# From the search on, every compute engine takes the program's order, laid out along a clock of products

## The chip, the cores and the metric

The kernel runs on one core of a Trainium2 chip. The metric is the device time of one execution in microseconds (us). The core's engines are TensorE (matrix products and transposes; PE in the profile, its weight loads PEld), VectorE (DVE), ScalarE (ACT), GpSimd (POOL) and SyncE (SP, which issues most transfers). Each has a queue of its own and they meet through semaphores.

## What is computed

Attention with 4 sink keys and a window of 128 keys (batch 4, 8 heads, 768 positions, head size 64) gives 3072 tokens of 512 numbers. A dense layer follows, and then a layer of eight experts. Cut to that:

```
h = x @ w_in                      # 512 -> 2048
x = (h - np.tanh(h)) @ w_out      # 2048 -> 512
logits = x @ w_gate               # one for each of 8 experts
# all (token, expert) pairs, greatest logit first:
#   give the token to the expert if the token is free and the expert has under 384
out[mask_e] = np.maximum(x[mask_e] @ w1[e], 0) @ w2[e]    # 512 -> 1024 -> 512
```

So each expert gets exactly 384 tokens, and which ones depends on all logits.

## The kernel before, in words

**Ahead of the change.** Tokens are handled in 8 units of 384. Attention and the dense layer run unit by unit, the second product of a unit beside the next unit's attention. Every fp32 operand of a large product is split into a rounded half and a remainder, and three products are summed: high by high, high by low, low by high. For the last unit, the logits are taken from the hidden values directly (`last_logits`, L476; `logits`, L434 to L438), so that the search can start before that unit's second product (`mlp_y`, L399 to L401) is done.

**The search.** `choose` (L1025 to L1040) finds for each token its greatest logit among the experts that are left and cuts it into eight digits of four bits. `search` finds, for the expert that fills first, the value of its 384th token, a digit a level, eight levels. In a level VectorE compares the digit with 16 steps, in two halves of 12 token columns (L648, L650, tile mk); TensorE counts by expert (six products, L655, into the bank `search`); VectorE takes the counts over (L665, csum); TensorE sums and spreads them (four products, L668); VectorE finds the digit (L673 to L677). Then `assign` writes the expert's number (L704, ei), the tokens' places (L706 to L742), two offset products (L711, L712), the one-hot tile `oh` in six pieces (L753), 24 products that gather the token numbers (L757), and the list `idx` (L759, L761). The next `choose` is issued in the middle of it, right after the offset products. One expert's search follows the other, as each needs the tokens left over; the eighth expert takes what remains.

**An expert.** Its number is read on SP's queue (L769), and 16 weight loads of 256 KB follow (L775, tile wraw, 8 buffers). ScalarE rounds each (L780), GpSimd takes the remainder (L782; for some of the first expert, VectorE). There are two sets of weights, so expert n + 2 loads where n has finished. GpSimd gathers the expert's 384 rows from memory (L789, yg), TensorE transposes them in four pieces of three (L794, xt), ScalarE and VectorE split them (L797, L798, mxh and mxl). `first` makes a slice of 128 hidden values with 12 products (L830 to L832), ScalarE and VectorE make hh and hl (L835, L836), `second` adds the slice to three result banks with 9 products (L846 to L848); eight slices an expert, `second` one slice behind. Results are copied (L852) and scattered (L853).

**What sets the order.** The instructions are traced in the program's order and then ordered by a scheduler that works with its own estimate of when each is ready. The program counts a clock of products (213 ns for each of L399 to L401, 480 for three of `first`, 640 for three of `second`), and `beside` lets the search go one step on whenever the clock reaches `due`, with gaps in `GAPS`. Each step's instructions of TensorE are tied behind the product just traced, and nothing else is tied: a later product may be scheduled ahead of a search product. `weights` paces loads (a quarter of `PACE0` or `PACE` apart) and their splits (`LAT`), and `step` places the transposes by `TW` and `TR`. The search may be one expert ahead of the next (`limit = n + 2`).

```
while due <= clock and chain:
    with tc.issue_after(mm.ins):
        gap = next(chain, None)
    if gap is not None:
        due = max(due, clock - 300) + gap
```

## Time and profile before

| | |
|---|---|
| median of 3 runs | 1261.08 us (1258.85 to 1264.31) |
| the profiled execution | 1260.94 us, of it span 1259.2 us |
| mean granted TensorE clock | 0.969 |
| busy: TensorE, weight loads | 92%, 76% |
| busy: VectorE, ScalarE, GpSimd | 62%, 51%, 41% |

The span goes from the first to the last instruction; what lies around it is 1.7 us. A matmul's end is modelled and matmuls overlap, so what one costs is read from start to start and not from its duration. A busy TensorE can still be slowed by changes between kinds of products. The stage that the change touches begins near 826.8 us, where the last unit's second product starts.

### The profile page before, as it was taken

The numbers are of one execution on the slowest core, as the hardware profiler recorded it, in microseconds if no ns is written. First come the engines' busy times: TensorE is split into PE (matmuls) and PEld (weight loads), VectorE is DVE, ScalarE is ACT, GpSimd is POOL, SyncE is SP. The second block draws the span as 40 slices with busy tenths as digits, with TensorE's granted clock in tenths as the row PEclk, the third lists the DMA queues.
The fourth block names the chain that finished last, engine by engine and source line by source line (L and its number), as shares of the span: only waits on it lengthen the run. The fifth ranks groups of instructions, "written<-read, shape, count | busy, mean of one in ns | idle before, by whom it ended". The sixth has DMA issues, their size and how long they took to land.

```text
span 1259.2 us, 19625 instructions
## 1 busy us (share of the span) xinstructions
PE 1160.1 (92%) x6484; PEld 954.4 (76%) x6484; DVE 780.1 (62%) x2205; ACT 642.6 (51%) x1556; POOL 513.9 (41%) x614
## 2 busy tenths in 40 slices
PE   4667899999999999999999999997899999999797
PEld 3556688888888788888888888875577777777696
DVE  6789985566665666655656654556667666667221
ACT  6876665666665567655656654412143244143411
POOL 6266753233442434432322331002174474484920
PEclk9868899999999999999999999999889999999999
DMA  6545552234333433432333221125154145145600
GB/s 218 176 145 181 187 163 93 76 104 132 108 110 111 134 107 107 131 104 67 100 98 91 91 82 48 37 59 187 49 167 144 60 159 169 57 151 170 190 26 26
DMA packets 87605, 145.28 MB, mean 115 GB/s; under 512 B 9680, under 2 KB 32208, under 8 KB 87504
## 3 DMA queue, kind: packets, MB, share of 16 engines
q1 hardware_dynamic: 83664, 131.45, 33.2%
q0 software_dynamic: 3840, 12.59, 3.0%
q8 instruction: 51, 0.84, 0.3%
q14 instruction: 50, 0.41, 0.1%
HBM read 127.22 MB, written 16.78 MB: 114 GB/s over the span
## 4 chain that ended last, share of the span: by engine, by line
PE 65%; DMA 7%; DVE 5%; issue 4%; ACT 2%; POOL 2%; SPq 1%; POOLq 0%; ACTq 0%; DVEq 0%
PE h L373 6%; PE y L401 6%; PE h L371 6%; PE h L372 6%; PE y L399 6%; PE y L400 6%; PE o L349 4%; PE h L830 3%; PE h L831 3%; PE h L832 2%; PE o L847 2%; PE o L848 2%; PE o L846 2%; DMA wraw<-in_w_dram 2%; PE t L317 2%
## 5 line engine op out<-in xcount | busy, mean ns | idle before, releaser
L782 POOL TENSOR_TENSOR w<-wraw,w 128x512 fp32r<-128x512 f32 x120 | 152.1, 1299 | 150.5 <-ACT w L780 122.1
L371 PE MATMUL h<-xh,win 128*128 128x384 f32 x512 | 178.6, 350 | 0.3 <-ACT xh L361 0.3
L373 PE MATMUL h<-xh,win 128*128 128x384 f32 x512 | 177.3, 346 | 0.0
L372 PE MATMUL h<-xl,win 128*128 128x384 f32 x512 | 175.2, 342 | 1.7 <-DVE xl L362 1.7
L401 PE MATMUL y<-wo,gl 128*128 128x512 f32 x336 | 141.3, 422 | 0.0
L399 PE MATMUL y<-wo,gh 128*128 128x512 f32 x336 | 135.1, 404 | 1.5 <-ACT gh L384 1.5
L400 PE MATMUL y<-wl,gh 128*128 128x512 f32 x336 | 136.2, 405 | 0.1
L298 POOL TENSOR_SCALAR a<-a,stat 128x260 f32<-128x260 f32 (+2 forms) x168 | 94.2, 573 | 80.0 <-DVE stat L290 74.2
L780 ACT CAST w<-wraw 128x512 fp32r<-128x512 f32 x128 | 78.1, 620 | 87.6 <-DMA wraw<-in_w_dram 83.5
L286 ACT ACTIVATE a<-sm,stat 128x260 f32<-128x260 f32 (+2 forms) x192 | 94.5, 492 | 41.3 <-DVE stat L285 39.1
L285 DVE CUSTOM_DVE_ANT_0 sm<-s,m 128x260 f32<-128x260 f32 (+2 forms) x192 | 76.8, 401 | 50.2 <-PE s L277 41.2
L371 PEld LDWEIGHTS h<-xh,win 128*128 128x128 f32 x512 | 97.5, 191 | 7.2 <-ACT xh L361 1.2
L372 PEld LDWEIGHTS h<-xl,win 128*128 128x128 f32 x512 | 97.6, 191 | 7.0 <-DVE xl L362 2.5
L378 DVE TENSOR_TENSOR g<-h,g 128x384 f32<-128x384 f32 x128 | 71.2, 556 | 47.7 <-ACT g L377 47.0
L248 POOL TENSOR_TENSOR kl<-k,kh 128x388 fp32r<-128x388 f32 (+1 forms) x64 | 81.4, 1279 | 45.1 <-ACT kh L247 45.1
L373 PEld LDWEIGHTS h<-xh,win 128*128 128x128 f32 x512 | 97.7, 191 | 2.5 <-issue 1.5
L835 ACT ACTIVATE hh<-h 128x384 fp32r<-128x384 f32 x64 | 31.2, 489 | 132.1 <-PE h L832 119.2
L377 ACT ACTIVATE g<-h 128x384 f32<-128x384 f32 x128 | 61.9, 484 | 66.8 <-PE h L373 61.7
L262 POOL TENSOR_TENSOR vs<-vr,vs 128x192 fp32r<-128x192 f32 (+1 forms) x64 | 46.5, 734 | 113.8 <-ACT vs L261 113.1
L830 PE MATMUL h<-mxh,w 128*128 128x384 f32 x256 | 91.1, 357 | 1.7 <-ACT mxh L797 1.7
L831 PE MATMUL h<-mxl,w 128*128 128x384 f32 x256 | 90.5, 354 | 0.0
L832 PE MATMUL h<-mxh,w 128*128 128x384 f32 x256 | 89.0, 348 | 0.0
(263 smaller groups left out, 2863.1 us busy)
## 6 DMA issues: line engine op xcount, KB each, us to landing
wl<-wol_d SPq DMA_DIRECT2D x128, 256.0 KB, 2.9
wraw<-in_w_dram SPq DMA_DIRECT2D x128, 256.0 KB, 3.9
k<-in_k_dram SPq DMA_DIRECT2D x64, 131.0 KB, 2.9
winr<-in_w_in_dram SPq DMA_DIRECT2D x8, 1024.0 KB
wor<-in_w_out_dram SPq DMA_DIRECT2D x8, 1024.0 KB, 4.9
wtr<-in_w_outT_dram SPq DMA_DIRECT2D x8, 1024.0 KB, 6.1
k<-in_k_dram SPq DMA_DIRECT2D x64, 97.0 KB, 2.5
q<-in_q_dram SPq DMA_DIRECT2D x32, 192.0 KB, 2.7
```

Source lines behind the costliest of these rows:

```text
L286: nc.scalar.activation(a[:, hh, :n], sm[:, :n], AF.Exp, bias=r[:, 0, hh:hh + 1], scale=-1.0, accum_out=r[:, 1, hh:hh + 1])
L298: nc.gpsimd.tensor_scalar(a[:, j, :n], a[:, j, :n], r[:, 3, j:j + 1], 1.0, op0=OP.mult, op1=OP.mult)
L371: nc.tensor.matmul(hp, w, xh[:, c], start=(c == 0), stop=False)
L372: nc.tensor.matmul(hp, w, xl[:, c], start=False, stop=False)
L373: nc.tensor.matmul(hp, win(f, 1, c), xh[:, c], start=False, stop=(c == NC - 1))
L399: yield 213, nc.tensor.matmul(y, gh[:, ts], hi, start=(f == 0), stop=False)
L400: yield 213, nc.tensor.matmul(y, gh[:, ts], lo, start=False, stop=False)
L401: yield 213, nc.tensor.matmul(y, gl[:, ts], hi, start=False, stop=(f == NF - 1))
L782: (dve if n == 0 and q % 2 else nc.gpsimd).tensor_sub(t[:, 1], r, raw(t)[:, 0])
L830: nc.tensor.matmul(hp, w1h[:, c], xh[:, c], start=(c == 0), stop=False)
L831: nc.tensor.matmul(hp, w1h[:, c], xl[:, c], start=False, stop=False)
L832: yield 480, nc.tensor.matmul(hp, w1l[:, c], xh[:, c], start=False, stop=(c == NC - 1))
```

## The change

All instructions of TensorE, VectorE, ScalarE and GpSimd that are traced from the search's pools on are chained in the program's order, engine by engine (`in_order`); SP's are not. The program's order is now laid out by a clock in ns with a heap of events: `advance` adds a product's cost (230 for the dense second product and `second`, 175 for `first`) and runs what is due. The clock keeps for VectorE, ScalarE and GpSimd until when each is taken (`on_vec`, `on_act`, `on_pool`). A search step yields four numbers: VectorE's time beside the products just issued, the lag from those products, VectorE's time for the step, and the cost of the products that come next; the next step runs when VectorE's time is over. hl, weight halves, result copies and scatters are events as well, and in `second` the three low products come last.

A level's comparison is one instruction and no longer two. The number is written before the places are worked out. The list comes ahead of the next choice. The digits are made as 1 + d/16 by integer operations on VectorE, where ScalarE scaled them before. The rows are gathered as soon as the list is there, and the transposes are placed 9500 ns later (`GOT`), and not before 28000 ns into the running expert (`TW`); a piece may wait up to 1500 ns for a search product to stand beside. The search may run three experts ahead of the running one's number (`limit = n + 3`, where it was `n + 2`). Loads are 2000 ns apart in the dense product and 1500 after it.

```diff
-PACE0, PACE = 5000, 6000
-LAT0, LAT = 5000, 6000
-TW, TR = (16000, 14000, 12000), 2000
-GAPS = (1600, 500, 1500, 6000)
+PACE0, PACE, LAT = 2000, 1500, 6500
...
-                yield 213, nc.tensor.matmul(y, gl[:, ts], hi, start=False, stop=(f == NF - 1))
...
+                    mm = nc.tensor.matmul(y, m[:, ts], w, start=(f == 0 and w is hi and m is gh),
+                                          stop=(f == NF - 1 and m is gl))
+                    yield 230, mm
...
     psH = ctx.enter_context(tc.tile_pool(name="psH2", bufs=2, space=bass.MemoryType.PSUM))
...
+    begin = len(nc.cur_bb.bb.instructions)
+    def in_order():
+        last = {}
+        for i in nc.cur_bb.bb.instructions[begin:]:
+            if i.engine in (mybir.EngineType.PE, mybir.EngineType.DVE, mybir.EngineType.Activation, mybir.EngineType.Pool):
+                if i.engine in last:
+                    tc.add_manual_dep(i, last[i.engine].name, mybir.DependencyInfo(
+                        mybir.DependencyClass.NoSync, mybir.DependencyReason.DATA), reason="in_order")
+                last[i.engine] = i
...
-            h = NJ // 2
-            for j in (0, h):
...
-                if l == 0:
-                    dve.tensor_tensor(mk[:, js], zb, kb, op=OP.is_ge)
...
-            yield GAPS[0] if l else 700
+            zb, kb = z[:, l, :, None].to_broadcast([P, NJ, 16]), K["steps"][:, None, :].to_broadcast([P, NJ, 16])
+            if l == 0:
+                dve.tensor_tensor(mk, zb, kb, op=OP.is_ge)
+            else:
+                dve.scalar_tensor_tensor(mk, zb, d, kb, op0=OP.subtract, op1=OP.is_ge)
+            yield 0, 100 if l else 0, 1200 if l else 530, 600
...
-            yield GAPS[1]
+            yield 350, 100, 200, 400
...
+        number(n, em)
+        yield 0, 100, 1150, 0
...
-        yield GAPS[2]
...
+        yield 0, 0, 1150, 300
...
-        if n < E - 1:
-            e1 = e1S
...
-            choose(nc, wk, KP, lm, *nxt, val=valH, dg=dgH)
...
-        yield GAPS[3]
+            yield 0, 0, 600, 0 if j + w < NJ else 1200
...
-        yield 1500
+        yield 0, 100, 400, 0
+        tokens()
+        if n < E - 1:
...
+            nxt = NXT[n + 1] = (bestH[n % 2], wk.tile(V3, BF, name="ch"), zH)
+            for dur in choose(nc, wk, KP, lm, *nxt, val=valH):
+                yield 0, 0, dur, 0
...
+            yield 0, 0, 350, 0
...
+    def advance(dt):
+        nonlocal clock
+        clock += dt
+        load()
+        while events and events[0][0] <= clock:
+            heapq.heappop(events)[2]()
+    def wait(ready):
+        while not ready():
+            advance(50)
...
+    def on_vec(t, dur):
+        nonlocal vec
+        vec = max(vec, t) + dur
+        return vec
...
+    steps, at, cost, limit = assign(0, *NXT[0]), 0, 0, 1
+    def search_step():
+        nonlocal clock, steps, cost
+        now = clock
+        clock += cost
+        r = next(steps, None)
+        if r is None:
+            steps = None
+            next_search()
+            return
+        before, lag, dur, cost = r
+        if before:
+            on_vec(now, before)
+        if clock > now and turns:
+            turns.pop(0)()
+        when(on_vec(clock + lag, dur) + (100 if cost else 0), search_step)
+    def next_search():
+        nonlocal steps, at, cost
+        if steps is None and at + 1 < E and at + 1 <= limit:
+            at, cost = at + 1, 0
+            steps = assign(at, *NXT[at])
+            when(vec, search_step)
...
+    def load():
+        nonlocal paced, raws
+        while (coming and clock >= paced and raws < 8 and coming[0][:2] in free and coming[0][0] in EI
+               and (coming[0] < (0, 2) or WPB)):
+            n, q, a = coming.pop(0)
+            load_w(n, q, a)
+            raws += 1
+            paced = clock + (PACE if WPB else PACE0)
+            when(clock + LAT + (1500 if q + a == 0 else 0), lambda n=n, q=q, a=a: split_hi(n, q, a))
+    def split_hi(n, q, a):
+        nc.scalar.copy(W[n, q][:, 0, a], WR[n, q, a])
+        when(on_act(clock, 620) + 80, lambda: split_lo(n, q, a))
+    def split_lo(n, q, a):
...
-        with tc.issue_after(GOT[n].ins) if q > 1 and n else ExitStack():
-            (dve if n == 0 and q % 2 else nc.gpsimd).tensor_sub(t[:, 1], r, raw(t)[:, 0])
...
+        (dve if mine else nc.gpsimd).tensor_sub(t[:, 1], r, raw(t)[:, 0])
...
+        n = gathered + 1
+        if not WPB or n == E or n not in IDX or (n and n - 1 not in XT):
+            return
+        gathered = n
...
+        when(clock + GOT, lambda: turn_all() if n == 0 else turn(n, 0))
...
+    def turn(n, c, asked=None):
+        nonlocal clock
+        asked = clock if asked is None else asked
+        if c == 0 and (running < n - 1 or clock < begun + TW):
+            when(clock + 200, lambda: turn(n, 0))
+            return
+        if steps and cost and clock < asked + 1500:
+            turns.append(lambda: turn(n, c, 0))
+            return
+        yg, xh, xl = HALF[n] if c else halves(n)
...
+        for i in range(NT):
+            nc.tensor.transpose(t[:, i * P:(i + 1) * P], yg[:, i, c * P:(c + 1) * P], ident)
+        clock += 500 if asked else 350
...
-            yield 480, nc.tensor.matmul(hp, w1l[:, c], xh[:, c], start=False, stop=(c == NC - 1))
+            for k, (h, x) in enumerate(((0, xh), (0, xl), (1, xh))):
+                nc.tensor.matmul(hp, w[:, h, c, fs], x[:, c], start=(c + k == 0), stop=(c == NC - 1 and k == 2))
+                advance(175)
...
-    def second(n, f, hh, hl):
...
-            yield 640, nc.tensor.matmul(o, hl[:, ts], w2h, start=False, stop=(f == NF2 - 1))
...
+            for k, w in enumerate((w2h, w2l)):
+                nc.tensor.matmul(o, hh[:, t * P:(t + 1) * P], w, start=(f + k == 0), stop=False)
+                advance(230)
+        wait(lambda: made)
+        for t, o in enumerate(O[n]):
+            nc.tensor.matmul(o, hl[:, t * P:(t + 1) * P], w2h, start=False, stop=(f == NF2 - 1))
+            if f == NF2 - 1:
+                res.append(t)
+                when(clock + 400, lambda t=t, o=o: store(n, t, o))
+            advance(230)
...
+    when(0, search_step)
+    advance(0)
...
-        for dt, mm in mlp_y(NU - 1, *((f,) if f < NF - 2 else (f, f + 1))):
-            beside(dt, mm)
-            weights()
+        for dt, _ in mlp_y(NU - 1, *((f,) if f < NF - 2 else (f, f + 1))):
+            advance(dt)
...
-    weights()
+    wait(lambda: 0 in IDX)
...
-        beside(200, mm)
...
-        limit = n + 2
-        if n and n not in XT:
-            finish(n - 1)
+        limit = n + 3
+        next_search()
+        if n not in XT and prev:
+            second(*prev)
...
+        wait(lambda: n in XT)
+        running, begun = n, clock
...
+    in_order()
...
+    yield 900
...
-    nc.vector.tensor_scalar(dg, sh, 15, None, op0=OP.bitwise_and)
-    nc.scalar.activation(z, dg, AF.Copy, scale=0.0625)
...
+    for ls, op in ((slice(0, 3), OP.logical_shift_right), (slice(3, 8), OP.logical_shift_left)):
...
+        nc.vector.tensor_tensor(dg[:, ls], u[:, 1:2].to_broadcast(D), K["shift"][:, ls, None].to_broadcast(D), op=op)
+    nc.vector.tensor_scalar(z.bitcast(I32), dg, 15 << 19, 127 << 23, op0=OP.bitwise_and, op1=OP.bitwise_or)
+    yield 1400
...
```

## Rows read from the trace of the kernel before

**Rows 1.** Busy time by stage: us, each engine (x instructions), TensorE clock, DMA share, GB/s
```profile
826.80:877.70 50.90, 47.19 (x263) 30.71 (x261) 30.13 (x140) 8.58 (x17) 5.64 (x6) 0.97 0.41 132
877.70:892.50 14.80, 5.74 (x43) 3.72 (x43) 11.16 (x34) 4.74 (x9) 8.85 (x7) 0.57 0.56 172
892.50:1170.00 277.50, 269.85 (x1683) 204.37 (x1682) 184.84 (x774) 98.46 (x186) 149.17 (x127) 0.99 0.39 126
1170.00:1215.30 45.30, 39.12 (x199) 33.21 (x198) 9.38 (x19) 15.79 (x31) 29.43 (x25) 0.96 0.35 109
1215.30:1259.20 43.90, 35.65 (x178) 31.83 (x176) 5.84 (x10) 6.28 (x12) 5.82 (x6) 0.96 0.10 36
```

**Rows 2.** Timeline of TensorE, one slice of an expert: start, us, instruction
```profile
1055.42 0.33 PE L830 MATMUL h<-mxh,w 128*128 128x384 f32 x1
...
1057.52 0.39 PE L846 MATMUL o<-w,hh 128*128 128x512 f32 x1
...
1059.60 0.33 PE L830 MATMUL h<-mxh,w 128*128 128x384 f32 x1
```

**Rows 3.** Timeline of TensorE around three and around six comparison products
```profile
1040.47 0.34 PE L831 MATMUL h<-mxl,w 128*128 128x384 f32 x1
1040.74 0.26 PE L655 MATMUL search<-mk,ch 128*32 128x64 bf16 x3
...
1041.21 0.34 PE L830 MATMUL h<-mxh,w 128*128 128x384 f32 x1
...
1066.22 0.34 PE L831 MATMUL h<-mxl,w 128*128 128x384 f32 x1
1066.49 0.35 PE L655 MATMUL search<-mk,ch 128*32 128x64 bf16 x6
...
1067.05 0.34 PE L830 MATMUL h<-mxh,w 128*128 128x384 f32 x1
```

**Rows 4.** Waits of TensorE, 892.5 to 1170: total us, times, longest
```profile
PE xt L794 <- DMA yg<-y_d,idx: 6.3, 7, 1.3
```

**Rows 5.** Waits of TensorE, 1170 to 1215.3
```profile
PE o L846 <- ACT hh L835: 4.5, 2, 2.4
```

**Rows 6.** Timeline of ScalarE beside expert 6; in brackets idle time before and what ended it
```profile
1192.80 0.62 ACT L780 CAST w<-wraw 128x512 fp32r<-128x512 f32 x1 [7.51 <-DMA wraw<-in_w_dram]
```

**Rows 7.** Timeline of VectorE: a level of a search, and the list's end between searches
```profile
951.37 0.17 DVE L673 TENSOR_SCALAR_CACHE_REDUCE full<-search 128x15 f32<-128x15 f32 x1 [0.40 <-PE search L668]
...
952.03 0.74 DVE L650 SCALAR_TENSOR_TENSOR mk<-hold,d,steps 128x192 bf16<-128x192 f32 x2
...
954.74 0.17 DVE L673 TENSOR_SCALAR_CACHE_REDUCE full<-search 128x15 f32<-128x15 f32 x1 [0.69 <-PE search L668]
...
972.30 0.62 DVE L648 TENSOR_TENSOR mk<-hold,steps 128x192 bf16<-128x192 f32 x2
...
974.23 0.16 DVE L761 SCALAR_TENSOR_TENSOR idx<-search,ls 128x3 int32<-128x3 f32 x1
...
1018.20 0.35 DVE L648 TENSOR_TENSOR mk<-hold,steps 128x192 bf16<-128x192 f32 x1
```

**Rows 8.** Instructions by tile, VectorE: duration ns min/median/max, first and last start
```profile
L650 DVE SCALAR_TENSOR_TENSOR mk<-hold,d,steps x98: 404/410/420, 835.7 to 1140.0; 128x192 bf16<-128x192 f32 x98
...
L836 DVE SCALAR_TENSOR_TENSOR hl<-h,hh x64: 534/557/560, 896.9 to 1247.4; 128x384 fp32r<-128x384 f32 x64
```

**Rows 9.** Timeline of TensorE at the start of the stage
```profile
826.86 0.39 PE L399 MATMUL y<-wo,gsh 128*128 128x512 f32 x1
...
833.23 0.26 PE L655 MATMUL search<-mk,CH 128*32 128x64 bf16 x3
```

**Rows 10.** Timeline of TensorE and VectorE around the seam before the experts
```profile
869.07 0.50 PE L400 MATMUL y<-wl,gsh 128*128 128x512 f32 x1 [3.71 <-DMA wl<-wol_d]
...
881.10 0.68 DVE L403 COPY ys<-y 128x512 f32<-128x512 f32 x1
...
892.57 0.99 PE L830 MATMUL h<-mxh,w 128*128 128x384 f32 x2
```

More of the change, by code (lines that the diff above doesn't have):

```diff
@@ L1 @@
+import heapq
 from contextlib import ExitStack
@@ new lines, in when, with on_act @@
+    def when(t, fn):
+        heapq.heappush(events, (t, next(order), fn))
+    def advance(dt):
[11 more added lines that the diff above has]
+        return vec
+    def on_act(t, dur):
+        nonlocal act
+        act = max(act, t) + dur
+        return act
@@ L791, in gather @@
-        xh = ep.tile([P, NC, CAP], F32R, name="mxh")
-        xl = ep.tile([P, NC, CAP], F32R, name="mxl")
-        def turn(t, c, i):
-            nc.tensor.transpose(t[:, i * P:(i + 1) * P], yg[:, i, c * P:(c + 1) * P], ident)
-        def split(t, c):
+            nc.gpsimd.indirect_dma_start(out=yg[:, t], out_offset=None, in_=y_d[:, :],
+                                         in_offset=bass.IndirectOffsetOnAxis(ap=IDX[n][:, t:t + 1], axis=0))
+        on_pool(clock, 3800)
+        HALF[n] = yg
@@ L818, in gather, with lo @@
-        XT[n] = (xh, xl)
-        yield
-    O = {}
+            clock += 350
+            on_vec(on_act(clock + 100, 480) + 60, 500)
+        XT[0] = xh, xl
+        tokens()
+    turns = []
+    def turn(n, c, asked=None):
+        nonlocal clock
+        asked = clock if asked is None else asked
[6 more added lines that the diff above has]
+        yg, xh, xl = HALF[n] if c else halves(n)
+        t = psS.tile([P, CAP], F32, name="xt")
+        for i in range(NT):
+            nc.tensor.transpose(t[:, i * P:(i + 1) * P], yg[:, i, c * P:(c + 1) * P], ident)
+        clock += 500 if asked else 350
+        nc.scalar.copy(xh[:, c], t)
+        def lo():
+            dve.tensor_sub(xl[:, c], t, raw(xh)[:, c])
+            e = on_vec(clock, 500) + 100
+            if c < NC - 1:
+                when(e, lambda: turn(n, c + 1))
+            else:
+                XT[n] = xh, xl
+                tokens()
+        when(on_act(clock + 100, 480) + 60, lo)
@@ L835, in first, with lo, second @@
         nc.scalar.activation(hh, hp, AF.Relu)
[L836 to L839 removed]
+        made = []
+        def lo():
+            dve.scalar_tensor_tensor(hl, hp, 0.0, raw(hh), op0=OP.max, op1=OP.subtract)
+            on_vec(clock, 500)
+            made.append(1)
+        when(on_act(clock + 200, 500) + 60, lo)
+        return hh, hl, made
+    res = []
+    def second(n, f, hh, hl, made):
@@ L840, in second @@
         if f == 0:
+            wait(lambda: not res)
             O[n] = [psY.tile([P, C], F32, name=f"o{t}", tag=f"y{t}") for t in range(NT)]
-        w = W[n, f // 4 * 2 + 1]
-        w2h, w2l = w[:, 0, f % 4], w[:, 1, f % 4]
+        q = f // 4 * 2 + 1
+        wait(lambda: split.get((n, q)) == NC)
+        w2h, w2l = W[n, q][:, 0, f % 4], W[n, q][:, 1, f % 4]
         for t, o in enumerate(O[n]):
-            ts = slice(t * P, (t + 1) * P)
-            nc.tensor.matmul(o, hh[:, ts], w2h, start=(f == 0), stop=False)
-            nc.tensor.matmul(o, hh[:, ts], w2l, start=False, stop=False)
-            yield 640, nc.tensor.matmul(o, hl[:, ts], w2h, start=False, stop=(f == NF2 - 1))
@@ L849, in second @@
-        if f == NF2 - 1:
-            for t, o in enumerate(O.pop(n)):
-                r = ep.tile([P, C], F32, name="res", bufs=3)
-                (dve.tensor_copy if t == 1 else nc.scalar.copy)(r, o)
-                d = nc.gpsimd.indirect_dma_start(
-                    out=out[:, :], out_offset=bass.IndirectOffsetOnAxis(ap=IDX[n][:, t:t + 1], axis=0),
-                    in_=r, in_offset=None)
-                for x in scat:
-                    tc.declare_no_dep(d.ins, x.ins, reason="every token has one expert")
-                scat.append(d)
@@ L862, in attn_mlp_moe @@
-    clock, due, limit = 0, 0, 1
-    chain, at = assign(0, *NXT[0]), 0
-    def beside(dt, mm):
-        nonlocal clock, due, chain, at
-        clock += dt
-        while due <= clock and chain:
-            with tc.issue_after(mm.ins):
-                gap = next(chain, None)
-            if gap is not None:
-                due = max(due, clock - 300) + gap
-            elif at + 1 < E:
-                if at + 1 > limit:
-                    due = clock
-                    return
-                at += 1
-                chain = assign(at, *NXT[at])
-            else:
-                chain = None
@@ L900, in attn_mlp_moe @@
-    next(chain)
+            for k, w in enumerate((w2h, w2l)):
[8 more added lines that the diff above has]
+            advance(230)
@@ new lines, in second, with store, out_rows @@
+        if f % 4 == 3:
+            free.add((n + 2, q))
+    def store(n, t, o):
+        r = ep.tile([P, C], F32, name="res", bufs=3)
+        if t == 1:
+            dve.tensor_copy(r, o)
+            e = on_vec(clock, 650)
+        else:
+            nc.scalar.copy(r, o)
+            e = on_act(clock, 600)
+        res.remove(t)
+        def out_rows():
+            d = nc.gpsimd.indirect_dma_start(
+                out=out[:, :], out_offset=bass.IndirectOffsetOnAxis(ap=IDX[n][:, t:t + 1], axis=0),
+                in_=r, in_offset=None)
+            on_pool(clock, 1000)
+            for x in scat:
+                tc.declare_no_dep(d.ins, x.ins, reason="every token has one expert")
+            scat.append(d)
+        when(e + 100, out_rows)
```

188 lines of the change are left out of this document (69 added, 119 removed).

## The prediction

> **What bounds the kernel now.** I first cut the end of the span by stages [rows 1]: the last unit's second product with the first search beside it (826.8 to 877.7), a seam (877.7 to 892.5), six experts with a search beside each (892.5 to 1170), expert 6 without one (to 1215.3), expert 7 and the way out (to 1259.2). The reader is to see that TensorE is at work 270 of 277.5 us in the six experts, 46.25 us each, but only 5.7 of 14.8 in the seam and 39.1 of 45.3 beside expert 6. What comes before 826.8 keeps its order and is not costed, but for the last choice (below).
>
> Second, what an expert costs by itself. In an undisturbed stretch of the timeline 12 first products take 2.10 us and 9 second ones 2.08 [rows 2], 4.18 us for one slice; eight slices are 33.4 us. So 12.8 of the 46.25 us are the search, the transposes and waits, though TensorE seems busy all the time. Third, the price of an interruption, read from starts: products that would be 0.175 us apart stand further apart with search products between them. Around three comparison products, L831 to the second next main product L830 is 0.74 us, 0.39 more than two products; around six in a row, 0.83, so 0.48 more [rows 3]. Six at once cost hardly more than three.
>
> Fourth, who waits: in the six experts TensorE waits 6.3 us for gathered rows [rows 4]; beside expert 6 it waits 4.5 us for hh [rows 5], which stands on ScalarE behind weight halves that wait for their transfer [rows 6]. The weights are late there because their expert's number comes late: search follows search at 45.9 us, 972.30 to 1018.20 [rows 7], as slow as the experts themselves. So TensorE's own time bounds the six experts, with the search right behind.
>
> **The change part by part, against the profiled execution's 1260.94 us** (span 1259.2, 1.7 around it; 0.14 under the median 1261.08).
>
> One comparison a level. Two comparisons on VectorE, 0.74 us together [rows 7], become one of twice the width; its cost lies between the 0.41 of one alone [rows 8] and 0.74. I take 0.58, the middle, since the second of a pair adds 0.33 and part of that is start-up. For TensorE two groups of three become one of six: 2 x 0.39 - 0.48 = 0.30 us a level, 2.4 us a search of eight levels, 14.4 us over the six searches beside experts and 2.4 for the first. [...] The rows, 0.39 for three and 0.48 for six, show a cost per interruption, and I go by them.
>
> The program's order. All four compute engines keep the order of a clock that charges 175 and 230 ns a main product (rows 2: 175 and 231). A search step's product is placed after the duration the plan gives its VectorE step, and if that is too short all of TensorE's queue stands behind it. Such hand-offs are 18 a search (8 comparisons, 8 counts, offsets, list), 108 in the six searches, 126 with the first. The plan leaves 1.4 us from count to comparison products; VectorE took 951.37 to 952.77, 1.40, with two comparisons and about 1.24 with one [rows 7]. I take 0.04 us a hand-off, 4.5 us; bounds 0 and 0.2 (22 us).
>
> Gather and transposes. The rows are asked for as soon as the list is there, and the transposes placed 9.5 us later, not before 28 us into the running expert; the 6.3 us of waiting [rows 4] go. The list's 24 products and the three transposes of a piece go in one group each: 0 to 1 us an expert, taken as 0. A little time at the lower clock level (the six experts show 0.99 [rows 1]) goes too: 1 us. Six experts: 277.5 - 14.4 - 6.3 - 1 + 4.5 = 260.3, or -17.2.
>
> List before next choice. The choice (some 3.3 us in the plan) moves behind the list. Before, the next search's first comparison began 1.9 us ahead of the list's end (972.30 and 974.23) [rows 7]. The list's expert gains, the next search starts later. I cost this at nothing, because TensorE at 43.4 us an expert covers it. Without that cover it is rival 1. The choice's last step goes from ScalarE to VectorE, worth some tenths at eight places, nothing beside the rest.
>
> Expert 6. The search may run three experts ahead, so the number and the weight transfers, 1.5 us apart, no longer wait for the last search. Each load still issues from SP's queue behind a read of the number, and each split still takes its turn on ScalarE and GpSimd; those engines were 35% and 65% busy there [rows 1]. 33.4 us plus two for the transposes: 35.3 instead of 45.3, -10. Bounds 0 and -11. Expert 7 and the way out: 43.9 as before.
>
> The start of the stage. Here program order costs. The stage's first product starts at 826.86, and the first comparison product ran at 833.23 [rows 9]; the products between filled the time of the last choice. The plan's clock knows nothing of that choice: it puts the comparison product after 530 + 100 ns, behind three products of 230. So TensorE stands from about 827.6 until the comparison is ready, and only the few small products of the last logits run meanwhile. Of the 6.4 us between the rows 0.7 are those three, 0.5 are won by the shorter choice and comparison, the small products take the rest above 4.5: cost 4.5 us; bounds 3, if more of the choice is hidden, and 7, if the clock falls to the lower level as well. Nothing hides it, for this stage too is TensorE's own.
>
> The rest of that stage: the wait of 3.7 us for a streamed weight half [rows 10], behind a burst of expert loads on SP's queue, now paced at 2 us instead of 1.25: 2.5 of it goes (bounds 0 and 3.7). With the search's 2.4 and 0.5 at the lower clock: 4.5 - 2.4 - 2.5 - 0.5 = -0.9.
>
> The seam. The last but one result tile is copied on VectorE at 881.10, 3.4 us after the stage's last product, behind weight halves and search steps; store, gather and transposes follow, first expert product 892.57 [rows 10]. In program order the copy stands right behind its products: -2.5, bounds 0 and -3.4.
>
> Sum: -0.9 - 2.5 - 17.2 - 10 = -30.6; 1260.94 - 30.6 = 1230.
>
> **Rivals.** (1) The search becomes the bound. A level now takes 951.37 to 954.74, 3.37 us [rows 7], and saves about 0.2 from the single comparison and some of TensorE's delay, but the whole choice joins the chain. If what the levels win goes into that, the pitch stays 45.9 and the six experts take 275.4: 15 of the 17.2 us are lost, 1245. For it: the chain is almost all VectorE and hl, mxl and res stand in the same queue. Against: in a level VectorE also waits for TensorE, 0.69 us ahead of 954.74 alone, and that gives room. 0.17.
>
> (2) Weights for expert 6 stay late, for SP, ScalarE and GpSimd are shared and ScalarE's order is now fixed: 1240. 0.13.
>
> (3) Slower: each search product stands in TensorE's queue before VectorE is done. Place: the 126 hand-offs; instead of letting a main product by, the engine stops. It decides from (30.6 + 4.5 + 6.3) / 126 = 0.33 us each; at 0.4 it is 50 us, so 1230 - 4.5 + 50 = 1276. For it: hl in VectorE's fixed order can hold a step for 0.56 us [rows 8], and longer where its hh is late. Against: the plan charges them too, and its durations are near the rows. 0.06. [...]
>
> (4) Grouping saves nothing: the 0.39 and 0.48 would be TensorE waiting for VectorE's next part and not the price of changing over. Then 14.4 and 2.4 stay away: 1247. 0.03, since the main products after the group are late as well, and no wait is shown there. [...]
>
> (5) The order was already as good as this, and the stops at seams give back the rest: 1261, 0.04.
>
> **The numbers.** Forecast 1230 with 0.57, rivals 0.17, 0.13, 0.06, 0.03, 0.04. Low end: no hand-off cost (-4.5), list and transposes grouped (-5), the wait for the streamed half all gone and the last microseconds at seam and expert 6 (-4): 1216. High end: 1250 takes in rivals 1, 2 and 4 and, short of those, half the upper bound of the hand-offs. A difference under 0.5% (6.3 us) is no change for this kernel. Faster: the forecast, rivals 2 and 4 and nearly all of rival 1, 0.88; no change 0.06; slower 0.06.
>
> **What would show it.** Comparison products in sixes with about 0.48 us around them; six experts at 43 to 44 us; expert 6 at 35 to 36 and no wait for hh; TensorE stopped for some 4 us before the stage's first comparison product; the seam near 12 us. Wrong would be: experts still 46 us apart with TensorE waiting for mk or csum (rival 3) or for gathered rows (rival 1), or expert 6 waiting for weights (rival 2).

## The result, and the profile after

The changed kernel takes 1231.42 us (median of 4 runs, 1229.73 to 1233.87); the kernel before took 1262.59 on the same chip. The ratio is 0.9759, 95% interval 0.9728 to 0.9789: 2.4% faster, some 30 us. The profiled execution took 1233.87 us, its span 1232.2.

The same view by stages as [rows 1] (us, busy time of each engine, TensorE's granted clock, DMA share, GB/s):

```profile
827.40:878.60 51.20, 46.58 (x273) 31.70 (x271) 32.19 (x139) 6.31 (x12) 5.21 (x5) 0.93 0.43 139
878.60:893.70 15.10, 6.16 (x53) 4.92 (x52) 9.39 (x38) 3.82 (x8) 5.54 (x5) 0.56 0.45 141
893.70:1152.30 258.60, 252.01 (x1680) 204.87 (x1678) 196.37 (x730) 95.83 (x190) 158.34 (x134) 0.98 0.45 141
1152.30:1187.40 35.10, 35.10 (x182) 31.56 (x181) 7.23 (x13) 12.58 (x25) 22.41 (x19) 1.00 0.30 97
1187.40:1232.20 44.80, 35.73 (x178) 31.84 (x176) 5.99 (x11) 6.08 (x12) 5.79 (x6) 0.92 0.09 36
```

| stage | before | after | difference | forecast |
|---|---|---|---|---|
| second product beside the first search | 50.9 | 51.2 | +0.3 | -0.9 |
| seam | 14.8 | 15.1 | +0.3 | -2.5 |
| six experts with searches | 277.5 | 258.6 | -18.9 | -17.2 |
| expert 6 | 45.3 | 35.1 | -10.2 | -10 |
| expert 7 and the way out | 43.9 | 44.8 | +0.9 | 0 |

The rows sum to -27.6; with the 0.6 us by which the first stage begins later, the spans differ by 27.0. The time came from two stages alone. The first two were meant to give something and gave nothing.

**Who waits now.** TensorE's waits from 893 to 1152.4, the answer to [rows 4]:

```profile
PE search L728 <- DVE r L724: 6.6, 1, 6.6
```

The 6.3 us for gathered rows are gone. None of the hand-offs of the search's levels appears, where the prediction had charged 4.5 us. One wait is left, a single stop of 6.6 us that the prediction did not know. Expert 6, which stood 4.5 us for hh [rows 5], shows no wait.

**The stop in expert 5.** Timelines of VectorE, then of GpSimd, at that place:

```profile
1124.28 0.13 DVE L708 TENSOR_SCALAR ei<-hold 1x1 int32<-1x1 f32 x1
1124.34 7.88 DVE L718 TENSOR_SCALAR S<-done 128x24 f32<-128x24 f32 x1
1132.17 0.08 DVE L719 MEMSET S<- 128x24 f32 x1
```

```profile
1123.84 0.95 POOL L903 DMA_INDIRECT yg<-y_d,idx  x1 [0.30 <-issue]
1124.80 7.39 POOL L883 TENSOR_TENSOR w<-wraw,w 128x512 fp32r<-128x512 f32 x6
```

L718 is a tiny instruction (24 numbers in each partition, SBUF to SBUF), and takes 7.88 us. It ends at 1132.22, with GpSimd's six weight halves, which end at 1132.19. Behind it in VectorE's order stands r, and for r the offset products that the plan has put into TensorE's order. The same instruction took 0.61 us in the kernel before, where it stood beside the second of two weight halves and ended, again, with it (at 1151.05; the half at 1151.02):

```profile
1150.44 0.61 DVE L701 TENSOR_SCALAR S<-done 128x24 f32<-128x24 f32 x1
```

**The start of the stage.** Timeline of TensorE, as in [rows 9]; in brackets the idle time before and what ended it:

```profile
827.94 0.40 PE L400 MATMUL y<-wo,gsl 128*128 128x512 f32 x1
829.02 0.35 PE L478 MATMUL s<-gsh,WPS 128*16 128x384 f32 x1 [0.68 <-ACT gsh L384]
829.61 0.35 PE L478 MATMUL s<-gsl,WPS 128*16 128x384 f32 x1 [0.25 <-DVE gsl L385]
830.52 0.35 PE L435 MATMUL llt<-ident,llr 16*128 16x16 f32 x3 [0.56 <-ACT llr L432]
833.56 0.50 PE L666 MATMUL search<-mk,CH 128*32 128x64 bf16 x6 [2.69 <-DVE mk L659]
833.99 0.80 PE L400 MATMUL y<-wo,gsh 128*128 128x512 f32 x1
```

Three main products, the small products of the last logits, then nothing until the comparison is ready: the stop as forecast, 0.68 + 0.25 + 0.56 + 2.69 = 4.2 us. But the main product behind it takes 0.80 where it took 0.40 before the stop. The window behind the stop says why:

```profile
833.90:839.00 5.10, 5.10 (x23) 3.18 (x20) 1.72 (x8) 0.00 (x0) 0.00 (x0) 0.50 0.17 48
```

TensorE works all of these 5.1 us at a granted clock of 0.50. Main products in a row start 0.43 us apart in it (835.94 to 838.08), and 0.23 apart ahead of the stop (827.49 to 827.94). By the clock half of the 5.1 us is lost, an estimate of 2.6 us (2.4 by those starts). In the kernel before the clock stayed at 1.00 through this stretch:

```profile
833.00:839.00 6.00, 6.00 (x38) 3.60 (x37) 3.17 (x18) 0.00 (x0) 0.00 (x0) 1.00 0.25 85
```

**A level.** The one comparison, by its line on VectorE (min/median/max in ns), the answer to [rows 8]:

```profile
L661 DVE SCALAR_TENSOR_TENSOR mk<-hold,d,steps x49: 617/618/619, 836.1 to 1104.3; 128x384 bf16<-128x384 f32 x49
```

It takes 0.62 us, not the 0.58 taken. From its first count product to the next level's, a level's median is 3.08 us (3.76 before), and search follows search at 40 to 41 us instead of 46.

### The profile page after: what moved, and what is told of

Same layout as the page of the kernel before. It is cut to its first block, busy times and chain, and to the rows that moved or that the text cites. A ratio compares the mean times of both kernels' runs of the same rounds, so it can differ in the third digit from the quotient of the medians.

```text
span 1232.2 us, 19570 instructions
## 1 busy us (share of the span) xinstructions
PE 1136.0 (92%) x6484; PEld 953.5 (77%) x6484; DVE 791.0 (64%) x2164; ACT 633.5 (51%) x1541; POOL 511.8 (42%) x615
## 4 chain that ended last, share of the span: by engine, by line
PE 72%; DVE 4%; DMA 4%; issue 3%; ACT 2%; POOL 1%; SPq 0%; POOLq 0%; DVEq 0%; ACTq 0%
PE y L400 18%; PE h L968 10%; PE o L995 6%; PE h L373 6%; PE h L371 6%; PE h L372 6%; PE o L349 4%; PE o L999 3%; PE t L317 2%; DMA wtr<-in_w_outT_dram 2%; PE s L276 2%; PE s L277 1%; PE search L666 1%; PE xt L945 1%; PE o L427 1%
## 5 line engine op out<-in xcount | busy, mean ns | idle before, releaser
L968 PE MATMUL h<-mxh,w 128*128 128x384 f32 x512 | 149.6, 350 | 0.0
L995 PE MATMUL o<-w,hh 128*128 128x512 f32 x384 | 106.4, 403 | 0.0
L968 PEld LDWEIGHTS h<-mxh,w 128*128 128x128 f32 x512 | 94.2, 191 | 3.5
L877 ACT CAST w<-wraw 128x512 fp32r<-128x512 f32 x128 | 72.7, 619 | 35.9 <-DMA wraw<-in_w_dram 35.6
```

Source lines behind the costliest of these rows:

```text
L877: nc.scalar.copy(W[n, q][:, 0, a], WR[n, q, a])
L968: nc.tensor.matmul(hp, w[:, h, c, fs], x[:, c], start=(c + k == 0), stop=(c == NC - 1 and k == 2))
L995: nc.tensor.matmul(o, hh[:, t * P:(t + 1) * P], w, start=(f + k == 0), stop=False)
```

## The experiments

Each differs from the changed kernel by the edit shown, unless said otherwise.

**1. The ones in PSUM.** Is it the form of L718, beside GpSimd's weight halves, that makes it slow?

```diff
-            dve.tensor_scalar(S[:, 0], done, -1.0, 1.0, op0=OP.mult, op1=OP.add)
+            dve.scalar_tensor_tensor(S[:, 0], done, -1.0, oneS[:, :NJ], op0=OP.mult, op1=OP.add)
```

> Against the changed kernel (1231.4 us) one instruction differs: 1 - done for the eighth expert is made with two sources, the second of them ones held in PSUM, and no longer with constants alone. In the changed kernel's trace it takes 7.88 us (L718) and ends with a burst of six remainders on GpSimd (1124.80 to 1132.19); TensorE waits 6.6 us for the offsets behind it and then runs about 3 us at the lower clock level. Theory (the one-source form has to wait for GpSimd, and program order puts TensorE behind it): it takes under 1 us, the wait goes, 7 to 8 us faster, about 1224. Rival (VectorE waits there for something else, such as the tile done): it stays at 7 to 8 us, 1231.

Measured: 1225.71 us (1223.16 to 1229.09), ratio 0.9733 (0.9701 to 0.9765). VectorE's timeline, then GpSimd's:

```profile
1122.02 0.16 DVE L718 SCALAR_TENSOR_TENSOR S<-done,search 128x24 f32<-128x24 f32 x1
```

```profile
1121.52 0.95 POOL L903 DMA_INDIRECT yg<-y_d,idx  x1 [0.30 <-issue]
1122.48 15.00 POOL L883 TENSOR_TENSOR w<-wraw,w 128x512 fp32r<-128x512 f32 x12
```

Now twelve weight halves follow in a row, and the instruction takes 0.16 us. It stands where it stood: beside the issue of a gather, and 0.46 us ahead of the row (1122.02 and 1122.48; 1124.34 and 1124.80 in the changed kernel). The stop is gone, and expert 5 takes 36.5 us instead of 44.9. So the form of the instruction, beside GpSimd's work, was the cause, and not VectorE's load. The edit changes the operation and the place of its second operand together; which of the two frees it is not shown. Other runs below keep the old form. Beside weight halves it took 5.93 us (experiment 3) and 2.64 (experiment 5), and ended 0.04 us behind the last half of the row both times. It is not held at every place: in experiment 2 it took 0.33 us beside the issue of a gather, and in experiment 6 0.16 beside that of a scatter. Why a row of halves holds the old form is not shown. The gain over many executions is less sure: the profile is 10.7 us shorter (8.4 of it in expert 5, and 2.2 from ahead of the stage, which begins at 825.28 instead of 827.49), the ratios differ by 0.0026 (3.3 us), and the intervals overlap.

**2. The plan told of the last choice.**

```diff
-    clock, vec, act, pool = 0, 0, 0, 0
+    clock, vec, act, pool = 0, 4600, 0, 0
```

> Against the changed kernel VectorE counts as taken for the first 4.6 us of the clock (the last unit's choice), so that the first comparison product is placed after about 22 main products and not after three. Theory (the stop at the start is the plan not knowing of the choice): TensorE's stops between 827.9 and 833.6, 4.2 us of them shown as waits, and the stretch at the lower clock after them go, 4.5 to 7 us faster, 1225 to 1227. Rival (the stage is held by the streamed weight halves or by the search, so that time saved at its start is waited out before its end): under 1.5 us.

Measured: 1222.81 us (1222.41 to 1225.29), ratio 0.9707 (0.9677 to 0.9738). The first stage by windows:

```profile
825.80:868.50 42.70, 42.47 (x257) 29.43 (x255) 26.94 (x121) 4.51 (x9) 5.21 (x5) 1.00 0.45 146
```

42.7 us instead of 51.2, at clock 1.00 instead of 0.93. In the changed kernel the stop and the small products in it add 5.8 us (827.94 to 833.99, less the 0.23 of a main product); here the same small products stand one by one between main products and add 1.2 by their starts. The stop thus costs 4.6 us, and the lower clock behind it 2.6 by the estimate above: 7.2, not 4.5. The rest of the 8.5 is no gain; 1.0 of it is products of the second search, which now come behind this stage.

But expert 1 now starts 50.0 us after expert 0 instead of 44.5: counted from the stage's start, expert 0 comes 8.6 us sooner, expert 1's list only 2.8, and expert 5 only 1.5. The total fell for another reason. L718 took 0.33 us in this run and stopped nothing, and expert 5 took 36.6 us instead of 44.9: that is 8.3 of the 11.4 us by which this profile is shorter, and 1.7 lie ahead of the stage. So the theory holds for the stage, and the total lies in its range by luck: most of what the start gives is waited out behind it.

**3. Two groups of products a level.** The comparison stays one.

```diff
-            yield 0, 100 if l else 0, 1200 if l else 530, 600
+            yield 0, 100 if l else 0, 1200 if l else 530, 300
...
+                if g == 2:
+                    yield 0, 0, 0, 300
```

> Against the changed kernel the six comparison products of a level are placed as three and three with a main product between, with one comparison on VectorE as now. Theory (a group costs by its place and not by its length: 0.39 us for three, 0.48 for six): 0.30 us a level, 8 levels, six searches beside experts and most of the first: 14 to 17 us slower, 1246 to 1248. Rival (the next weights are loaded while the present product runs, so that a group costs only its own products): under 3 us.

Measured: 1249.86 us (1248.89 to 1255.98), ratio 0.9932 (0.9908 to 0.9956): 0.0173 above the changed kernel, 21.8 us, give or take 5. The six experts by windows:

```profile
893.70:1171.40 277.70, 270.14 (x1706) 210.73 (x1704) 196.71 (x743) 93.32 (x185) 152.67 (x129) 0.97 0.41 128
```

19.1 us more than in the changed kernel, and TensorE is "busy" for 270 of the 277.7: a change of products leaves no idle row, it is read from the starts. Not all of the 19.1 is grouping. Nine more products of `second` fall into this window, 2.1 us, and waits and the lower clock add some 2.4. The price is clearest in an expert with one whole search beside it, no wait and clock 1.00; one of this run, then one of experiment 2:

```profile
1034.83:1079.57 44.74, 44.74 (x288) 34.37 (x286) 31.25 (x124) 15.19 (x31) 25.97 (x23) 1.00 0.42 130
```

```profile
1061.94:1104.38 42.44, 42.44 (x287) 34.14 (x286) 31.76 (x127) 15.30 (x30) 25.82 (x22) 1.00 0.43 137
```

2.3 us for eight levels are 0.29 a level; I had 0.30. Three products cost 0.39 us by the starts here too, though one comparison makes all six ready at once. Rival 4, by which grouping saves nothing, falls. Weight loads do run beside products (34.14 us of them in the last row, where products fill all 42.44), and going over to six short products and back still costs 0.48 us ([rows 3] and the changed kernel).

**4. Without the chain.** The plan still lays out the program; the scheduler may reorder it.

```diff
-    in_order()
```

> Against the changed kernel the chain that keeps the program's order on the four engines is left out; clock, single comparison and all else stay, and the scheduler orders by its own estimate, without the ties of a search step to a main product that the kernel before had. Theory (grouping and the early list bring most of the gain, the chain little): 1225 to 1240, with the start's stop and the 6.6 us wait for the offsets gone or smaller. Rival (the chain is what lets the plan hold): 1250 or more, with comparison products in other groups than six and TensorE waiting for VectorE.

Measured: 1270.7 us (1267.34 to 1271.86), ratio 1.0084 (1.0054 to 1.0114): slower than before. My theory, that the layout itself brings most of the gain, falls. TensorE's waits from 883.4 on, then GpSimd's timeline at one gather:

```profile
PE xt L945 <- DMA yg<-y_d,idx: 30.0, 7, 5.1
PE o L995 <- ACT hh L974: 2.1, 1, 2.1
```

```profile
1063.53 5.06 POOL L883 TENSOR_TENSOR w<-wraw,w 128x512 fp32r<-128x512 f32 x4
1068.72 0.98 POOL L903 DMA_INDIRECT yg<-y_d,idx  x1
```

The list is written at 1064.38, and the gather stands behind four weight halves until 1068.72. The first transpose of those rows has been put into TensorE's queue ahead of search products, and TensorE stands 4.7 us for it; the next search's products stand behind it too. Searches follow each other at 49 to 50 us, as slow as the experts. This is rival 1's outcome, and with this layout the chain is what keeps it out.

**5. The choice ahead of the list again.**

```diff
+            e1 = e1S
+            dve.tensor_scalar(e1, es, em, None, op0=OP.is_equal)
...
         mine, pos = mineS, posS
...
         tokens()
         if n < E - 1:
-            e1 = e1S
-            dve.tensor_scalar(e1, es, em, None, op0=OP.is_equal)
...
```

> The choice of the next expert is moved back ahead of the list; all else as changed. Theory (prediction: the place of the choice costs nothing, TensorE covers it): the list and the gather come 3 to 4 us later behind each search, the rows still arrive before the transposes, the pitch of the searches stays 40 to 41 us: 0 to +3 us against the changed kernel, ratio to before 0.975 to 0.980. Rival (list first is what keeps the rows from being late): TensorE waits for gathered rows again, 1 us or more an expert, +6 to +20 us, ratio 0.981 to 0.992.

Measured: 1231.45 us (1228.99 to 1235.3), ratio 0.9776 (0.9736 to 0.9816). A list takes 14.6 us from the expert's number instead of 11, searches keep their 40 to 41, and beside the experts TensorE waits for no gathered row; its waits there are 1.5 us for r, 1.2 for a count and 0.9 for a comparison. The six experts take 254.4 us instead of 258.6, since the stop behind L718 is only that 1.5 us. The five experts ahead of the stop take 216.5 us instead of 213.8, so 2.7 us is what the place of the choice can cost in the profile, within the theory's 0 to 3. It is little, as the prediction had it, given a plan that leaves room for the gather.

**6. Products placed too early.** Every search step that ends in products is planned 400 ns shorter.

```diff
         before, lag, dur, cost = r
+        dur = max(0, dur - 400) if cost else dur
```

> Every search step that ends in a TensorE product is planned 400 ns shorter, so that its product stands earlier in the program's order. Theory (a product placed before VectorE is done stops all of TensorE; the changed kernel has only some 0.1 to 0.4 us to spare at each of 126 places): TensorE shows waits for mk and csum beside the experts, 5 to 20 us in sum, and the time is 8 to 20 us more than the changed kernel's, ratio 0.982 to 0.992. Rival (the place of a product in the order hardly matters, the gain is the grouping): 0 to +3 us, 0.975 to 0.979.

Measured: 1234.38 us (1233.27 to 1239.39), ratio 0.9805 (0.9765 to 0.9846): 5.8 us above the changed kernel, between theory and rival, and not apart from either by its interval. Timeline of TensorE around one comparison:

```profile
960.25 0.33 PE L969 MATMUL h<-mxl,w 128*128 128x384 f32 x1
960.70 0.34 PE L666 MATMUL search<-mk,ch 128*32 128x64 bf16 x6
960.97 0.62 PE L969 MATMUL h<-mxh,w 128*128 128x384 f32 x2
```

The comparison products start 0.45 us after the last main product, not 0.27 as in [rows 3], and no wait is marked. Between products of `first` an interruption by six products costs 0.65 us in the median (0.48 in the changed kernel, and 0.48 in [rows 3]); one by the four count products stays at 0.39. So placing a comparison 0.4 us earlier costs 0.17, which leaves some 0.23 us to spare in the changed kernel, and more at a count. Experts 1 and 2 take 47.8 and 49.0 us (42.7 and 40.4), with more of the search beside them: a level takes 2.44 us from count to count (3.08), expert 6's number is written 31.8 us earlier, counted from the stage's start, and experts 4 and 5 run with little or none beside them (36.5 and 34.9 instead of 43.3 and 44.9).

The 5.8 us are too little for the price of the early products. This run has no stop behind L718 (0.16 us), which took 8.4 us of the changed kernel's expert 5 (experiment 1). An estimate with these added is 14 us, within the theory's range, though the sign that it named is weaker: the waits marked for mk and csum beside the experts are 2.7 us, and the rest shows only in the starts.

**7. Expert 0's transposes piece by piece.**

```diff
-        for c, t in enumerate(ts):
-            for i in range(NT):
+        for i in range(NT):
+            for c, t in enumerate(ts):
                 nc.tensor.transpose(t[:, i * P:(i + 1) * P], yg[:, i, c * P:(c + 1) * P], ident)
+        for c, t in enumerate(ts):
```

> Expert 0 alone: its transposes go piece by piece of gathered rows and not column by column, so that the first two pieces can be transposed before the third has come. Theory (the seam gained nothing because all twelve transposes stand behind the last piece): expert 0's first product 1 to 1.5 us sooner after the third gather than in the changed kernel, the seam 13.6 to 14.1 us instead of 15.1. Rival (the seam is set by the store and the gather alone): the seam stays 15 us.

Measured, in one run: 1230.34 us. TensorE's timeline in the changed kernel, then in this one:

```profile
888.24 0.45 PE L921 MATMUL xt<-ident,yg 128*128 128x128 f32 x1 [1.08 <-DMA yg<-y_d,idx]
889.58 0.48 PE L921 MATMUL xt<-ident,yg 128*128 128x128 f32 x1 [0.89 <-DMA yg<-y_d,idx]
891.02 2.39 PE L921 MATMUL xt<-ident,yg 128*128 128x128 f32 x10 [0.97 <-DMA yg<-y_d,idx]
```

```profile
885.70 1.08 PE L921 MATMUL xt<-ident,yg 128*128 128x128 f32 x4 [0.69 <-DMA yg<-y_d,idx]
887.00 1.11 PE L921 MATMUL xt<-ident,yg 128*128 128x128 f32 x4 [0.22 <-DMA yg<-y_d,idx]
888.43 1.12 PE L921 MATMUL xt<-ident,yg 128*128 128x128 f32 x4 [0.32 <-DMA yg<-y_d,idx]
```

Ten of twelve transposes stood behind the third piece; now four do. The seam is 13.6 us instead of 15.1. The theory holds for 1.5 us, and the rest of the seam is store and gather, as below.

**8. The single comparison alone,** in the kernel before: its own order, the choice ahead of the list, `limit = n + 2`.

```diff
-            h = NJ // 2
-            for j in (0, h):
+            h = NJ
+            for j in (0,):
```

> The kernel before with one part of the change alone: one comparison of double width a level, whose six products then stand in one group; no program order, the choice still ahead of the list, the search two ahead. Theory (prediction: 0.30 us a level of TensorE's time goes, 2.4 us a search, seven searches): up to -17 us; TensorE still waits for gathered rows and for expert 6's weights, so -8 to -17 us, ratio 0.987 to 0.994. Rival (without the program's order the time goes into other waits, since the search is almost as slow as the experts): 0 to -4 us, ratio 0.997 to 1.000.

Measured: 1250.93 us (1244.64 to 1255.36), ratio 0.9905 (0.9872 to 0.9939), 12 us faster than before. By windows, the six experts and expert 6; then TensorE's waits in the first of them:

```profile
896.20:1173.50 277.30, 261.90 (x1694) 204.41 (x1694) 181.20 (x731) 104.45 (x198) 161.56 (x137) 0.98 0.43 136
1173.50:1208.10 34.60, 34.60 (x181) 31.44 (x180) 7.37 (x13) 9.71 (x20) 17.21 (x15) 1.00 0.22 68
```

```profile
PE xt L794 <- DMA yg<-y_d,idx: 7.9, 14, 2.0
PE search L757 <- DVE jc L749: 4.4, 2, 2.3
PE xt L794 <- DVE mxl L798: 1.9, 2, 1.6
```

The total is within the theory's range, and the theory is wrong. The six experts gain nothing (277.3 for 277.5): the products are in sixes at 0.48 us an interruption, TensorE's busy time falls by 8, and its waits grow from 7.4 to 14.7 us (the three rows and 0.5 for hl). Nearly all the gain is at expert 6, 34.6 instead of 45.3. Its number is written 41.6 us ahead of its first product (1131.9) instead of 25.8 (1144.1), so its weights are there.

**9. Three mended places and the tail together:** 1, 2 and 7, and in expert 7's last slice each result bank finished before the next.

```diff
+        if n == E - 1 and f == NF2 - 1:
+            wait(lambda: made)
+            for t, o in enumerate(O[n]):
+                ts = slice(t * P, (t + 1) * P)
+                for a, w, stop in ((hh, w2h, False), (hh, w2l, False), (hl, w2h, True)):
...
+            return
```

> Three mended places and the tail together: the ones of the last expert's step in PSUM, the plan's clock for VectorE starting 4.6 us late, expert 0's transposes piece by piece, and the last slice of the last expert finished result by result. Theory (the parts lie in different stretches and add up): -3 us for the ones, -6 for the start, -1 for the transposes, 0 to -1 for the tail against the changed kernel: 1219 to 1223 where before is 1260, ratio 0.966 to 0.970. Rival (what is won at the start is lost again where expert 1 waits for its rows, the more so when expert 0 starts sooner): 0.970 to 0.973.

Measured: 1222.76 us (1220.21 to 1225.59), ratio 0.9704 (0.9674 to 0.9733): no different from experiment 2 alone. The rival holds: expert 1 starts 50.2 us after expert 0. The ones bring nothing on top, since L718 took only 0.33 us in experiment 2. The tail is 43.8 us instead of 44.8.

**10. Expert 1's rows sooner,** on top of 9.

```diff
-        when(clock + GOT, lambda: turn_all() if n == 0 else turn(n, 0))
+        when(clock + (7200 if n == 1 else GOT), lambda: turn_all() if n == 0 else turn(n, 0))
...
-        if steps and cost and clock < asked + 1500:
+        if n > 1 and steps and cost and clock < asked + 1500:
```

> The run with everything mended, and expert 1's transposes asked for 7.2 us after its list instead of 9.5 and placed as soon as they can be, not one behind each search product. Theory (what the earlier start won was lost at expert 1, whose transposes were placed 10 us after the main products' end allowed): expert 1 starts 46 to 47 us after expert 0 instead of 50.2, the profile 3 to 4 us under that run's, ratio 0.967 to 0.969. Rival (the search that runs beside is the bound there, and the wait moves on to expert 2): no difference, ratio 0.970 to 0.972.

Measured: 1215.62 us (1213.34 to 1218.31), ratio 0.9634 (0.9602 to 0.9666), the fastest here; its interval lies below the changed kernel's. By windows, its first stage, seam and six experts:

```profile
824.70:868.50 43.80, 42.72 (x257) 29.36 (x255) 26.89 (x120) 4.50 (x9) 5.13 (x5) 1.00 0.46 144
868.50:882.00 13.50, 5.74 (x49) 4.50 (x48) 10.26 (x39) 3.60 (x8) 3.06 (x3) 0.59 0.67 214
882.00:1135.00 253.00, 251.58 (x1699) 203.85 (x1698) 192.74 (x748) 96.76 (x193) 160.87 (x136) 1.00 0.46 145
```

Expert 1 starts 44.3 us after expert 0, better than the 46 to 47 expected: what held it was where the plan put the transposes, not the rows. In run 9 TensorE had run out of main products there and stopped 4.0 us for counts and comparisons; here it shows no wait beside expert 0. The rival's wait does move on, but small: expert 2 starts 45.3 us after expert 1, 1.8 more than in run 9, and expert 3 follows in 40.4, 2.9 less.

## Why the prediction was right, and where its steps were not

The forecast of 1230 us is 1.4 us from the median, and against the profiled execution 3.9 us too low: stage by stage it had 3.6 us too much gain, of the 30.6. Some of its terms are right for the wrong reason, and the closeness is in part luck. The six experts gave 18.9 for 17.2, but without the stop behind L718 (1) they give 27.3:

```profile
891.51:1141.71 250.20, 250.20 (x1679) 203.32 (x1678) 188.46 (x730) 95.69 (x190) 158.34 (x134) 0.99 0.46 146
```

Worked out from the starts, the search's products with lists and transposes cost 18 us less (14.4 forecast, with lists and transposes taken as 0), waits 7.4 less (6.3), the lower clock 2.1 less (1), and the 4.5 for hand-offs were not paid. A stop of 8.4 us that no term had took most of that surplus back.

**Grouping** ("2 x 0.39 - 0.48 = 0.30 us a level", 16.8 us in all). The price per level is confirmed by both kernels' starts and by undisturbed experts, 0.29 us (3), and taking it back inside the program's order costs 21.8 us in all, give or take 5. But it is not a term that stands by itself. Made alone it leaves the six experts where they were (8), because what TensorE saves it then spends on waiting for rows and lists. The order with two groups a level leaves them there as well, 277.7 (3); by an estimate it would bring some 8 us without its own stop behind r (4.7 us of wait and the lower clock after it) and the nine products. Only both together give the 18.9 us, or 27.3 without the stop. That the sum missed this did no harm, as the change makes both.

**Expert 6** ("the search may run three experts ahead"). The size is right, -10.2 for -10, the reason is wrong. With the limit left at n + 2 the changed program lays out the same instructions in the same order: the limit never binds. The single comparison alone, with the old limit, frees the expert (8), and so does the plan with two groups a level, 34.9 us (3). What goes with it is how long ahead the number is written: 25.8 us before, 35.5 in (3), 41.6 in (8), 44.4 in the changed kernel. The pace of the loads, the number's place ahead of the token places and the integer digits were not tried by themselves; (8) has none of them and frees the expert all the same.

**Hand-offs** ("0.04 us, 4.5 us"). None shows: by an estimate from (6) the plan leaves 0.2 us of slack and more. Rival 3's mechanism exists, at 0.17 us a comparison for 0.4 us too early, but is far from the 0.33 a hand-off at which it would decide. In its place stood the stop behind L718, which no step of the prediction had: the fixed order let one slow instruction on VectorE hold all of TensorE. It took 6.6 us as a wait and 8.4 with the lower clock behind it (0.50 from 1132.80 to 1136.30); that 4.5 had been charged for something else is an accident.

**The start** ("cost 4.5 us; bounds 3 ... and 7"). The stop was seen where forecast, and by itself it cost what was forecast, 4.6 us (2). What the 4.5 left out is the lower clock behind it, by estimate 2.6 us, which the prediction had only in its upper bound: 7.2 in all. Against that the wait for the streamed half fell from 3.7 [rows 10] to 0.5 us, 0.7 more than the 2.5 taken, and some 1.3 us at the lower clock behind it (0.50 from 869.64 to 872.60 in the kernel before, 1.00 from 868 to 876 in the changed one) went, where 0.5 were taken. So the stage gave +0.3 for -0.9.

**The seam** ("the copy stands right behind its products: -2.5"). VectorE's copy does come 3.7 us earlier, at 877.41 for 881.10 [rows 10], and still the gather starts at 884.50 (884.67 before). SyncE's queue and GpSimd's first gather after the change:

```profile
878.12 1.59 SPq L406 DMA_DIRECT2D y_d<-ys  x2
880.28 2.65 SPq L796 DMA_DIRECT2D wraw<-in_w_dram  x3
```

```profile
884.50 1.16 POOL L903 DMA_INDIRECT yg<-y_d,idx  x1 [14.43 <-DMA wraw<-in_w_dram]
```

The last store is issued 2.4 us earlier, at 879.38 for 881.80, but the gather follows it by 5.1 us where it took 2.9 before. Fifteen of the store's sixteen parts had landed by 881.4, and the last one at 883.5, 1.0 us ahead of the gather; before, all sixteen landed from 883.6 to 883.8, 0.9 ahead of it. The row's bracket names a weight load, but the store's last part fits in both kernels. Loads stood beside it in both; why one part came so late was not tried. The transposes in column order cost 1.5 us more (7).

**List before choice** ("costed at nothing") holds to within 2.7 us (5), and is carried by the chain (4). **Rival 1**, the search as the bound, did not come: 40 to 41 us against an expert's 43, since a level lost 0.7 us, where the rival counted on about 0.2 and some of TensorE's delay. It lies close, as experiment 4 shows.

**The way out** (43.9 as before) is 0.9 us longer, since the low products of all three banks come last and so the three results are ready together; (9) gets it back.

## What to carry to other kernels

When a queue's order is fixed, a plan needs slack at each hand-off (0.4 us less cost 0.17 us a comparison), and needs to know all that the engines still have to do when it begins: one forgotten choice cost 7.2 us, of it an estimated 2.6 as clock. Two parts of a change that share a bound are not summed from prices: take one away from the end product and make one alone; here a part was worth 22 us by the first and 12 by the second, in another stage. A total can also fall, or stay, for a reason that the edit did not intend: L718's stop was gone or small in experiments 2, 5 and 6, whose edits have nothing to do with it. So read the stage that was edited before the total. And after each mended stop look at who is early now: the gain at the start only reached the end when the next expert's transposes were moved as well.

## What the runs showed of the hardware that was not expected

A VectorE instruction of 24 numbers a partition, SBUF to SBUF (L718), stood 7.88 us beside six GpSimd subtractions in a row, until the last of them ended, and took 0.16 us in experiment 1's form, with its second operand in PSUM, started just as far ahead of such a row. In the changed kernel a store of 0.33 us of issue had fifteen of its sixteen parts landed in 2 us and the last after 4.1. After 4.2 us of stops, in pieces, TensorE ran its next 5.1 us at a granted clock of 0.50, an estimated 2.6 us more.
